# Turning the local q and k in two tiles of five and four tokens, in a sparse attention and expert layer on one core

## The chip, the core and the metric

The kernel runs on one core of one Trainium2 chip. The core has a matrix engine (TensorE, PE in the profile, with its weight loads listed apart as PEld), three engines for elementwise work (VectorE or DVE, ScalarE or ACT, GpSimd or POOL) and an engine that mostly issues transfers (SyncE, SP). Matmuls and transposes write to PSUM, and ACT or DVE copy the result to SBUF. The metric is the device time of one execution in microseconds, the median over several runs; smaller is better.

## The reference

Two layers follow each other. The first is attention over 8 batches, 8 heads, 576 tokens and 64 features a head. Heads 0 to 3 are local (a query sees itself and the 31 keys before it); heads 4 to 7 are strided (a query sees earlier keys at a distance that is a multiple of 32). The second is a two-matmul layer over all 4608 tokens with a leaky activation whose slope `alpha` is given for each of 2048 features.

```python
scores = scale * np.matmul(q, k.transpose(0, 1, 3, 2))
rel = pos[:, None] - pos[None, :]
mask_local = (rel >= 0) & (rel < stride)                      # stride = 32
mask_strided = (rel >= 0) & (pos[None, :] % stride == pos[:, None] % stride)
scores = np.where(masks[None, :, :, :], scores, -1000000000.0)
attn = softmax(scores)
x = np.matmul(attn, v)                                        # heads side by side: (4608, 512)
h = x @ w_in                                                  # (4608, 2048)
g = np.maximum(h, 0.0) + alpha * np.minimum(h, 0.0)
return (g @ w_out).astype(np.float32)                         # (4608, 512)
```

## The kernel before, in words

A batch has four pairs of heads: pairs 0 and 1 are local, pairs 2 and 3 strided. Pair `g` of the whole kernel is pair `g % 4` of batch `g // 4`. For each pair the kernel computes scores (PE), exponentials (ACT), a mask, the product with v (PE, "PV"), a division by the row sum (a reciprocal and a multiplication on DVE), and a transposition of the result into `xT` (PE and a copy, or a DMA). The dense layer then works through nine chunks of 512 tokens: `lin1_piece` (L601: four matmuls of 512 columns into a buffer `hps`, a `neg` on ACT at L609, a `gT` on DVE at L612), and the second matmul (L640, L726, or `U` and `W` at L884 and L899 for the first chunk).

To compute scores, q and k have to lie with the features on the partitions, so they are turned. The local q and k of a batch arrive with nine consecutive tokens on each of 64 partitions per head half, are cast to 16 bit (`cast_l`), and are turned in one of two ways. Batches 0 to 4 use PE: nine transposes each, from one token of two heads each, in `transpose_piece` (L254, called `T(u, nm)`). Later batches use a DMA. The strided q and k go another way (`turn_first`, `turn_second`, or a DMA).

In `transpose_piece` eight tokens go into one PSUM tile `tp` of 2 KB a partition. The destination interleaves tokens: token `9 p + t` is column `9 p + t`, so a copy of eight tokens writes runs of eight adjacent columns and leaves one out. The ninth tokens of q and of k go together into a second tile, `tt`, after k's eight, and are copied by `tails` (L283): q's by DVE, k's by ACT. In batches 0 and 1 (`early`) the eight-token copy is cut by head pair in two halves for ACT and DVE; in batches 2 to 4 it is one ACT copy.

PSUM tiles come from pools with a fixed number of buffers in rotation. The pool `ps` has three, and `tp`, `tt`, the PV results, the turned outputs `xp` and some score tiles all take from it in program order; a new tile waits until the readers of the tile three places before it are done. The pool `hps` has three more, `sp` one.

Each engine works in the order in which the program records its instructions. For batch 0 and batch 1 this order is written out by hand as lists of small pieces (L843 and L910). `F` turns the strided q or k of a pair, `Sc(g, i)` computes half the scores of pair `g`, `Pv(g, a)` one group of PV, `X(g)` the transposition into `xT`, `T` the turn of the local q or k, `Cl` its cast on POOL, `vs` the cast of strided v, `ov` a copy inside the local v, `L(m)` the first half of a `lin1` piece, `w(n)` a number of warm-up matmuls that compute nothing (L768). From batch 2 on, attention pieces are fed one by one between the matmuls of the dense layer (L928), at a rate worked out from what is left.

Of the kernel before, what the change touches and what calls it, by code (L numbers as in the profile page):

```python
# [10 lines left out]
F16 = mybir.dt.float16  # L11
# [21 lines left out]
def kernel(  # L33
# [10 lines left out]
    nc = tc.nc  # L44
    keep = tc.keep_in_program_order
# [17 lines left out]
    pspool = ctx.enter_context(tc.tile_pool(name="ps", bufs=3, space=bass.MemoryType.PSUM))  # L63
# [10 lines left out]
    ident = consts[:, 0:128]  # L74
# [10 lines left out]
    qTs = [cpool.tile([128, 2, 672], F16, name=f"qT{i}") for i in range(2)]  # L85
    kTs = [cpool.tile([128, 2, 672], F16, name=f"kT{i}") for i in range(2)]
# [8 lines left out]
    cast16 = {}  # L95
# [109 lines left out]
    def cast_copy(eng, o, i):  # L205
        if eng == "act":
            keep(nc.scalar.copy(o, i))  # L207
        elif eng == "dve":
            keep(nc.vector.tensor_copy(o, i))  # L209
        else:  # L210
            keep(nc.gpsimd.tensor_copy(o, i))  # L211
# [9 lines left out]
    def over_v(b, eng, c0=0, c1=24):  # L221

        v16 = vls[b % 2]
        a = max(c0, 1)
        cast_copy(eng, v16[0:32, a:c1, :], v16[96:128, a - 1 : c1 - 1, :])
# [28 lines left out]
    def transpose_piece(u, nm):  # L254

        b = u // 2  # L260
        early = b < NEARLY
        src = cast16[(b, False, nm)]
        dst = qTs[u % 2][:, :, 0:576] if nm == "q" else kTs[u % 2][:, :, 32:608]
        tp = pspool.tile([128, 8, 64, 2], F16, tag="ps", name="tp")
        for t in range(8):
            keep(nc.tensor.transpose(
                tp[:, t].rearrange("r p e -> r (p e)"), src[:, t].rearrange("p f d -> p (f d)"), ident))
        main = tp.rearrange("r t p e -> r e p t")
        o = dst.rearrange("r e (p t) -> r e p t", t=9)[:, :, :, 0:8]
        if early:  # L270
            for e in range(2):
                eng = "dve" if (nm == "q") == (e == 0) else "act"
                if u == 0 and nm == "q":
                    eng = "act"
                if nm == "k" and e == 1:
                    tails(b, u)
                cast_copy(eng, o[:, e : e + 1], main[:, e : e + 1])
            return
        cast_copy("act", o, main)
        if nm == "k":  # L280
            tails(b, u)

    def tails(b, u):  # L283
        tt = pspool.tile([128, 2, 64, 2], F16, tag="ps", name="tt")
        for i, nm in enumerate("qk"):
            keep(nc.tensor.transpose(
                tt[:, i].rearrange("r p e -> r (p e)"),
                cast16[(b, False, nm)][:, 8].rearrange("p f d -> p (f d)"), ident))
        for i, (o, eng) in enumerate(((qTs[u % 2][:, :, 0:576], "dve"), (kTs[u % 2][:, :, 32:608], "act"))):
            cast_copy(eng, o.rearrange("r e (p t) -> r e p t", t=9)[:, :, :, 8],  # L290
                      tt[:, i].rearrange("r p e -> r e p"))

    def score_piece(P, i):

# [149 lines left out]
    def x_piece(P, eng):  # L444
        xp = pspool.tile([128, 1024], F16, tag="ps", name="xp")
        for t in range(P.n):
            keep(nc.tensor.transpose(  # L447
                xp[:, P.w * t : P.w * t + P.w], P.x16[0 : P.w, 128 * t : 128 * t + 128], ident[0 : P.w, 0 : P.w]))
# [44 lines left out]
    for g in range(7, npair + 2):  # L493
        c = g // 4
        a, p, t = g, g - 1, g + 1
# [269 lines left out]
    def warm(n):  # L765

        for _ in range(n):
# [12 lines left out]
            name=nc.get_next_instruction_name(), act_func_set_id=6, ins=[], outs=[]  # L780
# [35 lines left out]
    def F(nm, pr):  # L816
        return lambda: turn_first(nm, pr)
# [18 lines left out]
    def L(m):  # L836
        return lambda: lin1_piece(0, m, True)
# [3 lines left out]

    warm(17)
    for fn in [  # L843
        F("q", 0), w(1), F("k", 0), w(2), F("k", 1), Sc(2, 0), w(1), Sc(2, 1), alpha, w(1), F("q", 1), w(2),
        vs(0, 0), vs(0, 1), w(1), Pv(2, 0), Cl(0, "q"), Sc(3, 0), Pv(2, 2), Cl(0, "k"), Pv(2, 1), Sc(3, 1),
        Pv(3, 0), T(0, "q"), w(1), Pv(3, 2), w(1), X(2), T(0, "k"), w(1), Pv(3, 1), w(1), ov(0, "pool", 0, 12),
        Sc(0, 0), Sc(0, 1), X(3), Pv(0, 0), ov(0, "dve", 12, 24), Sc(1, 0), Pv(0, 1), Sc(1, 1), Pv(1, 0), L(0),
        Pv(1, 1), L(3), L(2), X(0, "act"), X(1), L(1)]:
        fn()
    load_d(1)  # L850
    load_v(1, True)
# [27 lines left out]
    def U(kf):  # L879
        def run():  # L880
            if kf == 0:
                banks.extend(phpool.tile([128, 512], F32, tag="hps", name="ops") for _ in range(3))
            for mt in range(3):
                keep(nc.tensor.matmul(  # L884
                    banks[mt], gTs[0][:, kf, 128 * mt : 128 * mt + 128], wout16[:, kf, :],
                    start=(kf == 0), stop=(kf == 15)))
            if kf == 15:
                for mt in range(3):
                    osb = opool.tile([128, 512], F32, tag="osb", name="osb")
                    cast_copy("dve" if mt == 1 else "act", osb, banks[mt])  # L890
                    keep(nc.sync.dma_start(out[128 * mt : 128 * mt + 128, :], osb))
        return run
# [14 lines left out]
    def sc1(g):  # L907
        return lambda: score_both(pairs[g], "dve")

    for fn in [  # L910
        U(0), Cl(1, "q"), G("k", 1), vs(1, 0), vs(1, 1), sc1(6), U(1), U(2), sc1(7), U(3), U(4), Cl(1, "k"), loads2,
        Pv(6, 0), Pv(7, 0), Pv(6, 2), U(5), Pv(7, 1), U(6), T(2, "q"), Pv(7, 2), U(7), T(2, "k"), U(8), Pv(6, 1),
        X(7, "dve"), W(0), W(1), sc1(4), U(9), W(2), sc1(5), W(3), ov(1, "dve", 0, 24), W(4), U(10), X(6), U(11),
        Pv(4, 1), W(5), Pv(4, 0), U(12), Pv(5, 1), U(13), U(14), Pv(5, 0), U(15), W(6), X(5), X(4), W(7)]:
        fn()
# [65 lines left out]
```

## Time and profile before

| what | value |
| --- | --- |
| median of 3 runs | 307.54 us (306.44, 307.66, 307.54) |
| profiled execution | 306.46 us, its span 304.5 us |
| PE busy | 294.4 us (97% of the span) |
| DVE, ACT, POOL busy | 223.4, 176.1, 175.6 us |
| granted clock of PE | 1.000 |
| batch 0's dense run of L601 begins | 24.96 us |

Times in the profile count from the start of the span. A row of the timeline has a start, a duration, the engine, the line and operation, the output and inputs, their shape and a count; behind it in brackets stands how long the engine was idle before it and what ended that wait. A row of the waits has an engine and its line, what it waited for, and total, number and longest in microseconds. A matmul's row ends when its result is in PSUM, by a model; the next matmul can start well before that.

### The profile page before, as it was taken

Reading aid. Unit: us, or ns where it says so; the run is one execution under the profiler, and the core shown is the slowest. Engines: PE = TensorE matmul, PEld = TensorE weight load, DVE = VectorE, ACT = ScalarE, POOL = GpSimd, SP = SyncE. Lnnn points to the kernel's source line nnn. Section 1 sums busy time; section 2 is a strip of 40 time slices with the busy share of each in tenths; the row PEclk is TensorE's granted clock in tenths of the full one; section 3 lists DMA queues with packets and bytes.
Section 4 is the critical chain, followed back from the end, with each engine's and each line's share of the span. In section 5 each row is a group of like instructions: output and inputs, shape, how many; then the busy total and the mean of one; then the engine's idle time right before and its main releaser. Section 6 shows DMA issues by size and latency. Waiting matters only on the chain.

```text
span 304.5 us, 6839 instructions
## 1 busy us (share of the span) xinstructions
PE 294.4 (97%) x2688; PEld 182.3 (60%) x2688; DVE 223.4 (73%) x413; ACT 176.1 (58%) x326; POOL 175.6 (58%) x163
## 2 busy tenths in 40 slices
PE   8989998999999998999999999999999999999995
PEld 3654454544555466845874587457745974685484
DVE  4567897758875888478948894889489948935852
ACT  1485744388557775577357746774575446426630
POOL 8362274128959997979897989394744404002300
PEclk9999999999999999999999999999999999999999
DMA  7999999999999998999989999955920040022003
GB/s 185 256 194 197 263 176 259 136 209 328 90 173 169 112 104 83 135 210 123 145 127 204 141 141 169 194 86 94 189 56 19 6 156 2 0 69 71 1 2 138
DMA packets 96976, 41.18 MB, mean 135 GB/s; under 512 B 75360, under 2 KB 93232, under 8 KB 96944
## 3 DMA queue, kind: packets, MB, share of 16 engines
q0 software_dynamic: 51008, 17.77, 57.3%
q1 hardware_dynamic: 45584, 22.32, 32.9%
q10 hardware_dynamic: 352, 0.66, 0.8%
q8 instruction: 21, 0.34, 0.5%
q14 instruction: 11, 0.09, 0.1%
HBM read 38.24 MB, written 9.44 MB: 157 GB/s over the span
## 4 chain that ended last, share of the span: by engine, by line
PE 79%; DVE 10%; ACT 6%; issue 2%; DMA 2%; SPq 0%; DVEq 0%; ACTq 0%
PE hps L601 36%; PE ops L726 24%; PE ops L640 4%; PE pv L424 4%; DVE gT L612 3%; DVE gsum L670 2%; PE sp L371 2%; PE ops L884 2%; DMA consts<-consts 2%; ACT neg L609 2%; DVE qT L209 1%; PE sph L371 1%; PE xp L447 1%; ACT kT L207 1%; PE ops L899 1%
## 5 line engine op out<-in xcount | busy, mean ns | idle before, releaser
L601 PE MATMUL hps<-xT,win 128*128 128x512 f16 x576 | 131.9, 379 | 0.2 <-ACT xT L470 0.2
L612 DVE SCALAR_TENSOR_TENSOR gT<-neg,oma,hps 128x512 f16<-128x512 f32 x144 | 105.3, 744 | 36.4 <-ACT neg L609 28.5
L609 ACT ACTIVATE neg<-hps 128x512 f32<-128x512 f32 x144 | 86.3, 601 | 34.7 <-PE hps L601 32.7
L601 PEld LDWEIGHTS <-win 128*128 128x128 f16 x576 | 53.8, 98 | 59.2 <-issue 0.7
L396 POOL TENSOR_TENSOR et<-et,consts 128x576 f16<-128x576 f16 (+1 forms) x24 | 34.7, 1447 | 35.4 <-ACT et L394 35.1
L670 POOL TENSOR_TENSOR gsum<-gT 128x1024 f16<-128x1024 f16 x14 | 29.7, 2124 | 42.2 <-DVE gT L612 37.2
L726 PEld LDWEIGHTS <-gsum 128*128 128x128 f16 x448 | 40.9, 98 | 7.3 <-DVE gsum L670 2.1
L726 PE MATMUL ops<-wsum,gsum 128*128 128x256 f16 x328 | 41.6, 273 | 0.4 <-DVE gsum L670 0.2
L726 PEld LDWEIGHTS <-gT 128*128 128x128 f16 x336 | 31.5, 98 | 5.4 <-issue 0.3
L433 DVE TENSOR_TENSOR x<-pv,rc 96x384 f16<-96x384 f32 (+2 forms) x62 | 33.0, 532 | 2.1
L403 POOL TENSOR_TENSOR et<-et,consts 128x576 f16<-128x576 f16 (+1 forms) x24 | 31.5, 1311 | 0.0
L424 PEld LDWEIGHTS <-et 72*128 72x128 f16 (+1 forms) x448 | 23.2, 98 | 12.5 <-issue 1.8
L726 PE MATMUL ops<-wout,gT 128*128 128x256 f16 x224 | 27.9, 272 | 0.1
L394 ACT ACTIVATE et<-sp 128x576 f16<-128x576 f32 (+1 forms) x24 | 15.6, 648 | 16.6 <-PE sp L371 16.6
L431 DVE RECIPROCAL rc<-pv 96x6 f32<-96x6 f32 (+2 forms) x80 | 14.6, 183 | 10.2 <-PE pv L424 10.2
L681 DVE TENSOR_TENSOR osb<-ops,par 128x512 f32<-128x512 f32 (+1 forms) x14 | 9.4, 672 | 16.1 <-PE ops L726 8.2
L400 ACT ACTIVATE et<-sph 128x288 f16<-128x288 f32 (+1 forms) x48 | 19.0, 413 | 0.0
L679 ACT COPY osb<-ops 128x512 f32<-128x512 f32 x14 | 8.2, 586 | 17.0 <-PE ops L726 16.9
L211 POOL COPY vs<-stv 72x1024 f16<-72x1024 f16 x12 | 13.4, 1118 | 6.7 <-DMA stv<-in_v_dram 6.7
L640 PE MATMUL ops<-wout,gT 128*128 128x512 f16 x64 | 16.4, 379 | 0.0
L424 PE MATMUL pv<-vs,et 72*128 72x65 f16 x256 | 15.2, 193 | 0.8 <-DVE vs L209 0.7
L743 ACT COPY par<-ops 128x512 f32<-128x512 f32 x13 | 8.0, 612 | 13.5 <-PE ops L726 13.5
(109 smaller groups left out, 342.2 us busy)
## 6 DMA issues: line engine op xcount, KB each, us to landing
out_dram<-osb SPq DMA_DIRECT2D x35, 256.0 KB, 3.4
vl<-in_v_dram POOLq DMA_DIRECT2D x6, 384.0 KB, 8.8
win<-in_moe_w_in_dram POOLq DMA_DIRECT2D x4, 512.0 KB, 16.8
wout<-in_moe_w_out_dram POOLq DMA_DIRECT2D x4, 512.0 KB, 17.7
qsd<-in_q_dram POOLq DMA_DIRECT2D x7, 288.0 KB, 5.9
ksd<-in_k_dram POOLq DMA_DIRECT2D x7, 288.0 KB, 7.0
stv<-in_v_dram POOLq DMA_DIRECT2D x7, 288.0 KB, 7.1
ql<-in_q_dram SPq DMA_DIRECT2D x3, 576.0 KB, 6.2
```

The source lines that it names most:

```text
L394: keep(nc.scalar.activation(ev.rearrange("r (y c) -> r y c", y=2), sp[0:r, :, 0:n], AF.Exp, scale=SCALE))
L396: keep(nc.gpsimd.tensor_tensor(mv, mv, m, op=ALU.mult))
L400: keep(nc.scalar.activation(ev[:, n * y : n * y + n], sps[y][0:r, 0:n], AF.Exp, scale=SCALE))
L403: keep(nc.gpsimd.tensor_tensor(mv, mv, m, op=ALU.mult))
L424: keep(nc.tensor.matmul(pv[:, 65 * x : 65 * x + 65], et[0:r, c : c + 128], v16[0:r, 2 * P.pr + hh, t, :] if P.strided else v16[:, 6 * (2 * ...
L433: keep(nc.vector.tensor_tensor(P.x16[0:w, c0 : c0 + 64 * nb].rearrange("r (c e) -> r c e", e=64), pvv[:, :, 0:64], rc[0:w, 0:nb].unsqueeze ...
L601: keep(nc.tensor.matmul(hps, win16[:, kk, 128 * m : 128 * m + 128], xT[:, kk, c0 : c0 + 512], start=(kk == 2), stop=(kk == 1)))
L609: keep(nc.scalar.activation(neg, hps, AF.Relu, scale=-1.0))
L612: keep(nc.vector.scalar_tensor_tensor(gTs[n][:, m, :], neg, oma[:, m : m + 1], hps, op0=ALU.mult, op1=ALU.add))
L640: keep(nc.tensor.matmul(ops, gTs[n][:, kf, 128 * mt : 128 * mt + 128], wout16[:, kf, :], start=(kf == 0), stop=(kf == 15)))
L670: keep((nc.vector if eng == "dve" else nc.gpsimd).tensor_tensor(gsum[i][:, hs], a, b, op=op))
L726: keep(nc.tensor.matmul(o, lhs(y), rhs(y), start=(first and y == 0), stop=(y == 7), skip_group_check=True))
```

## The change

Only the turn of the local q and k, and the written-out orders, are changed. `transpose_piece` now makes two `tp` tiles for each of q and k: the first holds tokens 0 to 4, the second tokens 5 to 8. Each tile is copied with one instruction, for both head pairs. The first copy is always ACT's. The second is ACT's too, except in batches 0 and 1, where DVE makes it (but ACT for the q of batch 0). `tails` and its tile `tt` are gone.

The list of batch 0 has another order, and seven warm-up matmuls between its pieces where there were twelve. In it v is cast earlier (`vs`), the score halves of pairs 3, 0 and 1 come in another order, `T(0, "k")` comes ahead of `Pv(2, 1)`, `X(3)` and `X(2)`, and X(2) and X(3) change places. In batch 1 one PV piece and `U(8)` change places.

```diff
-        tp = pspool.tile([128, 8, 64, 2], F16, tag="ps", name="tp")
-        for t in range(8):
-            keep(nc.tensor.transpose(
-                tp[:, t].rearrange("r p e -> r (p e)"), src[:, t].rearrange("p f d -> p (f d)"), ident))
-        main = tp.rearrange("r t p e -> r e p t")
-        o = dst.rearrange("r e (p t) -> r e p t", t=9)[:, :, :, 0:8]
-        if early:
-            for e in range(2):
-                eng = "dve" if (nm == "q") == (e == 0) else "act"
-                if u == 0 and nm == "q":
-                    eng = "act"
-                if nm == "k" and e == 1:
-                    tails(b, u)
-                cast_copy(eng, o[:, e : e + 1], main[:, e : e + 1])
-            return
-        cast_copy("act", o, main)
-        if nm == "k":
-            tails(b, u)
-
-    def tails(b, u):
...
+        o = dst.rearrange("r e (p t) -> r e p t", t=9)
+        tps = []
+        for t0, t1 in ((0, 5), (5, 9)):
+            tp = pspool.tile([128, 8, 64, 2], F16, tag="ps", name="tp")
+            for t in range(t0, t1):
+                keep(nc.tensor.transpose(
+                    tp[:, t - t0].rearrange("r p e -> r (p e)"), src[:, t].rearrange("p f d -> p (f d)"), ident))
+            tps.append(tp[:, 0 : t1 - t0].rearrange("r t p e -> r e p t"))
+        cast_copy("act", o[:, :, :, 0:5], tps[0])
+        cast_copy("dve" if early and (u or nm == "k") else "act", o[:, :, :, 5:9], tps[1])
...
-        F("q", 0), w(1), F("k", 0), w(2), F("k", 1), Sc(2, 0), w(1), Sc(2, 1), alpha, w(1), F("q", 1), w(2),
-        vs(0, 0), vs(0, 1), w(1), Pv(2, 0), Cl(0, "q"), Sc(3, 0), Pv(2, 2), Cl(0, "k"), Pv(2, 1), Sc(3, 1),
-        Pv(3, 0), T(0, "q"), w(1), Pv(3, 2), w(1), X(2), T(0, "k"), w(1), Pv(3, 1), w(1), ov(0, "pool", 0, 12),
-        Sc(0, 0), Sc(0, 1), X(3), Pv(0, 0), ov(0, "dve", 12, 24), Sc(1, 0), Pv(0, 1), Sc(1, 1), Pv(1, 0), L(0),
-        Pv(1, 1), L(3), L(2), X(0, "act"), X(1), L(1)]:
+        F("q", 0), w(1), F("k", 0), w(1), F("k", 1), Sc(2, 0), vs(0, 0), w(1), F("q", 1), Sc(2, 1), alpha, Pv(2, 0),
+        Sc(3, 1), vs(0, 1), Cl(0, "q"), Cl(0, "k"), Pv(2, 2), Sc(3, 0), w(1), Pv(3, 2), T(0, "q"), Pv(3, 0), w(1),
+        Pv(3, 1), w(1), T(0, "k"), X(3), w(1), Sc(0, 1), Pv(2, 1), Sc(0, 0), Sc(1, 1), ov(0, "dve", 12, 24),
+        ov(0, "pool", 0, 12), Pv(0, 1), X(2), Pv(0, 0), Sc(1, 0), Pv(1, 1), L(1), X(0, "act"), Pv(1, 0), L(2), L(3),
+        X(1), L(0)]:
...
-        Pv(6, 0), Pv(7, 0), Pv(6, 2), U(5), Pv(7, 1), U(6), T(2, "q"), Pv(7, 2), U(7), T(2, "k"), U(8), Pv(6, 1),
+        Pv(6, 0), Pv(7, 0), Pv(6, 2), U(5), Pv(7, 1), U(6), T(2, "q"), Pv(7, 2), U(7), T(2, "k"), Pv(6, 1), U(8),
```

More of the change, by code (lines that the diff above doesn't have):

```diff
@@ L263, in transpose_piece @@
         dst = qTs[u % 2][:, :, 0:576] if nm == "q" else kTs[u % 2][:, :, 32:608]
-        tp = pspool.tile([128, 8, 64, 2], F16, tag="ps", name="tp")
-        for t in range(8):
-            keep(nc.tensor.transpose(
-                tp[:, t].rearrange("r p e -> r (p e)"), src[:, t].rearrange("p f d -> p (f d)"), ident))
-        main = tp.rearrange("r t p e -> r e p t")
-        o = dst.rearrange("r e (p t) -> r e p t", t=9)[:, :, :, 0:8]
-        if early:
-            for e in range(2):
-                eng = "dve" if (nm == "q") == (e == 0) else "act"
-                if u == 0 and nm == "q":
-                    eng = "act"
-                if nm == "k" and e == 1:
-                    tails(b, u)
-                cast_copy(eng, o[:, e : e + 1], main[:, e : e + 1])
-            return
-        cast_copy("act", o, main)
-        if nm == "k":
-            tails(b, u)
-    def tails(b, u):
[L284 to L291, printed above, removed]
+        o = dst.rearrange("r e (p t) -> r e p t", t=9)
[8 more added lines that the diff above has]
+        cast_copy("dve" if early and (u or nm == "k") else "act", o[:, :, :, 5:9], tps[1])
     def score_piece(P, i):
```

## The prediction

> **What bounds the kernel now.** I read the page's first part, then the waits of TensorE alone, then the timeline around each of the five places where the local q and k are turned.
>
> ```profile
> span 304.5 us, 6839 instructions
> PE 294.4 (97%) x2688; PEld 182.3 (60%) x2688; DVE 223.4 (73%) x413; ACT 176.1 (58%) x326; POOL 175.6 (58%) x163
> ...
> PE 79%; DVE 10%; ACT 6%; issue 2%; DMA 2%; SPq 0%; DVEq 0%; ACTq 0%
> ```
>
> TensorE (PE) is busy for 97% of the span, and the other engines are not close to full. So only two things save time: less matmul work, or an end to a stall of PE. The waits of PE name the stalls (total, times, longest, in us):
>
> ```profile
> PE sp L371 <- ACT kT L207: 1.6, 3, 0.8
> ...
> PE sp L313 <- ACT kT L207: 1.0, 1, 1.0
> PE pv L424 <- DVE vs L209: 0.7, 1, 0.7
> PE xp L447 <- ACT kT L207: 0.7, 1, 0.7
> PE tt L286 <- ACT qT L207: 0.5, 1, 0.5
> ```
>
> Apart from the `vs` row, each of these waits ends at a copy out of a transpose tile, and these are the copies that the change rewrites. The groups of those copies (min/median/max in ns):
>
> ```profile
> L207 ACT COPY qT<-tp x6: 588/800/1016, 16.0 to 112.9; 128x512 f16<-128x512 f16 x3, 128x1024 f16<-128x1024 f16 x3
> L207 ACT COPY kT<-tt x5: 718/722/737, 18.6 to 118.7; 128x128 f16<-128x128 f16 x5
> L209 DVE COPY qT<-tt x5: 710/715/726, 17.9 to 118.0; 128x128 f16<-128x128 f16 x5
> L209 DVE COPY qT<-tp x1: 678/678/678, 46.3 to 46.3; 128x512 f16<-128x512 f16 x1
> ```
>
> A ninth token's copy moves 128 elements a partition and takes 0.72 us, more than the 0.59 us of 512 elements in runs of eight. It writes single 2-byte elements 18 bytes apart. So the price here is not by elements alone.
>
> **The price of one new copy.** It writes 128 runs (2 x 64) of five or four elements. Below stands the ninth token's copy, 128 runs of one at 0.72 us; above stands the old big copy, 128 runs of eight at 1.01 us. By elements alone, from 0.59 us at 512 and 1.01 at 1024 (0.82 ns each), 640 would take 0.69 and 512 would take 0.59 us. I take 0.75 us for either, since the ninth token's row has the same count of runs and lies nearest; the ends are 0.59 and 1.01. The same on DVE, whose row for the ninth token is 0.71.
> [...]
>
> **Batches 2 to 4 (one turn each).** Before, after k's eight transposes, three copies follow each other, the last two on one shared tile: k's eight tokens (ACT), q's ninth (DVE), k's ninth (ACT). The first scores wait for the last.
>
> ```profile
> 65.64 1.89 PE L601 MATMUL hps<-xT,win 128*128 128x512 f16 x8
> 65.78 1.01 ACT L207 COPY kT<-tp 128x1024 f16<-128x1024 f16 x1
> 67.32 0.72 ACT L207 COPY kT<-tt 128x128 f16<-128x128 f16 x1 [0.54 <-DVE qT L209]
> 68.09 0.30 PE L371 MATMUL sp<-qT,kT 64*128 64x96 f16 x6 [0.56 <-ACT kT L207]
> ...
> 85.93 1.01 ACT L207 COPY kT<-tp 128x1024 f16<-128x1024 f16 x1 [1.34 <-PE tp L266]
> 86.83 1.03 PE L640 MATMUL ops<-wout,gT 128*128 128x512 f16 x4
> 88.05 0.30 PE L371 MATMUL sp<-qT,kT 64*128 64x96 f16 x6 [0.19 <-ACT kT L207]
> ...
> 116.53 1.02 ACT L207 COPY kT<-tp 128x1024 f16<-128x1024 f16 x1
> 117.63 1.04 PE L726 MATMUL ops<-wsum,gsum 128*128 128x256 f16 x8
> 118.71 0.72 ACT L207 COPY kT<-tt 128x128 f16<-128x128 f16 x1 [1.16 <-DVE qT L209]
> 119.48 0.30 PE L371 MATMUL sp<-qT,kT 64*128 64x96 f16 x6 [0.82 <-ACT kT L207]
> ```
>
> A matmul row includes the last one's modelled tail, so a 512-wide matmul takes (1.89 - 0.38) / 7 = 0.216 us of PE, a 256-wide one (1.04 - 0.27) / 7 = 0.11. PE could have gone on at 65.64 + 8 x 0.216 = 67.37, at 86.83 + 4 x 0.216 = 87.69 and at 117.63 + 8 x 0.11 = 118.50. It went on at 68.09, 88.05 and 119.48: stalls of 0.72, 0.36 and 0.98, in sum 2.06 us. After, k's two ACT copies start where the one started and end 1.5 us on, at 67.3, 87.4 and 118.0, each ahead of the moment when PE is free. So all 2.06 us go. At 1.01 a copy they end at 67.8, 87.95 and 118.55, and 0.3 + 0.1 + 0.9 = 1.3 is left, less perhaps 0.3 for ACT work that queues behind q's copies.
> What it adds: ACT has 4 x 0.75 = 3.0 us a batch where it had 1.01 + 1.01 + 0.72 = 2.74, and DVE loses 0.71. ACT is at 58%, so the 0.26 us lie beside matmuls; the `neg` evictions behind q's copies come at most 0.5 us later, which the three rotating `hps` buffers cover (0.87 us of matmuls each). The eighteen transposes stay eighteen: zero. With these waits gone, the next thing late is a PV wait on DVE's eviction in batch 4, which stays.
>
> **Batch 1.**
>
> ```profile
> 46.32 0.68 DVE L209 COPY qT<-tp 128x512 f16<-128x512 f16 x1
> 47.03 0.59 ACT L207 COPY qT<-tp 128x512 f16<-128x512 f16 x1 [3.81 <-DVE qT L209]
> 47.67 0.22 PE L286 MATMUL tt<-consts,ql 128*128 128x128 f16 x1 [0.47 <-ACT qT L207]
> ...
> 48.33 0.89 DVE L209 COPY kT<-tp 128x512 f16<-128x512 f16 x1
> 48.74 0.72 ACT L207 COPY kT<-tt 128x128 f16<-128x128 f16 x1 [0.63 <-DVE qT L209]
> 49.51 0.42 PE L447 MATMUL xp<-consts,x 72*128 72x72 f16 x8 [0.74 <-ACT kT L207]
> ```
>
> Here ACT and DVE shared one tile and went one after the other. PE stalled twice: for the buffer of `tt`, and for that of `xp`. After, ACT takes five tokens and DVE four from different tiles, side by side. DVE still frees q's second tile first at 46.3 + 0.75 = 47.1, so k's second tile costs PE some 0.2 us. The PV piece that now stands ahead of U(8) takes its buffer from the one evicted behind that copy, some 0.4 us more. ACT is through with k's first tile by 48.0, so `xp` starts at about 48.6 and not 49.51: 0.9 us. Ends: 0.3 (copies of 1.01, two of them in DVE's queue) and 1.2 (both waits gone).
>
> **Batch 0.**
>
> ```profile
> 14.06 1.15 POOL L211 CAST kl<-kl 128x1152 f16<-128x1152 f32 x1 [1.00 <-DMA kl<-in_k_dram]
> 17.12 0.64 ACT L207 COPY xT<-xp 128x576 f16<-128x576 f16 x1
> 17.13 0.61 PE L266 MATMUL tp<-consts,kl 128*128 128x128 f16 x8
> 19.04 0.17 DVE L431 RECIPROCAL rc<-pv 72x6 f32<-72x6 f32 x1
> 19.24 0.55 DVE L433 TENSOR_TENSOR x<-pv,rc 72x384 f16<-72x384 f32 x1
> 19.41 0.30 PE L313 MATMUL sp<-qT,kT 64*128 64x96 f16 x6 [0.95 <-ACT kT L207]
> 24.96 11.04 PE L601 MATMUL hps<-xT,win 128*128 128x512 f16 x50
> ```
>
> The new order puts X(2) and PV(2,1) behind k's turn. K is cast at 14.06 + 1.15 = 15.2, so its transposes can stand at about 15.6 instead of 17.13 (q's two ACT copies free the buffer about then). With ACT's five tokens and DVE's four side by side, 0.75 each behind DVE's eviction of the last strided PV, kT is whole at some 17.1, and the first local scores stand there instead of at 19.41: 2.3 us earlier. The moved X(2) then costs ACT 0.64 us between there and the dense run; PV(2,1), 0.17 + 0.55 on DVE, has slack there, and is the lower end. That leaves 1.7, and 1.6 after the last X copy's wait. Ends: 2.3 (nothing moved counts) and 0.7 (PV counts, and some 0.2 of waits). The earlier `vs` cast stands ahead of q's second strided copy on DVE, so a late v would hold that copy and the scores behind it:
>
> ```profile
> 1.43 1.56 POOL L189 DMA_DIRECT2D stv<-in_v_dram  x2 [0.27 <-issue]
> ...
> DMA to landing us min/median/max: 8.5/9.1/9.7
> ```
>
> The first half lands at 1.43 + 8.5 = 9.9 us, about when DVE is ready for it; the second at about 12.0, by its place before the next eviction. Five warm-up matmuls fewer take 5 x 0.216 = 1.1 us of PE work out; it lay in stalls, so it counts nothing by itself. SP and POOL issue the same transfers in the same order, and POOL's own casts wait for landings that do not move.
>
> **The sum.** 1.6 + 0.9 + 2.06 = 4.6 us. Nothing behind these places gives it back by the profile: in the stages after 128 us PE runs without such waits and only shifts. The profiled execution took 306.46 us (span 304.5 and 2.0 around it): 301.9. The median of the runs shown is 307.54, 1.1 more: 303.0, which I predict.
>
> **The rivals.**
> *Dear copies.* Runs of four and five cost what runs of eight do, 1.01 us. For it: the ninth token's row shows a price by run. Against it: the row lies at the lower end. Gain 0.7 to 1.6 + 0.3 + 1.0, about 2.4: 305.1 us. Chance 0.12.
> *Batch 0 gives nothing*, because another wait (v, or ACT's exps) takes the place. Gain 2.9: 304.6. Chance 0.06.
> *A cold clock.* The opening shows PE at half rate:
>
> ```profile
> 5.01 0.15 PEld L768 LDWEIGHTS <-wrm 128*128 128x128 f16 x1 [0.28 <-issue]
> 5.43 1.22 PEld L768 LDWEIGHTS <-wrm 128*128 128x128 f16 x6 [0.28 <-issue]
> ```
>
> Starts are 5.43 - 5.01 = 0.42 us apart there, then 0.2. With fewer warm-up matmuls the clock could fall back for a spell as long as that opening, some 4 us, at about 1.7 us of cost beyond the stalls: 304.7. Against it: PE never stalls for over 1 us in the prologue. Chance 0.04. [...]
> *Slower: the ring of three `ps` buffers.* Each turn now holds two of three at once, and twice in a batch; before, a batch took three tiles, now four. If PE stood at the second tile of each of the ten turns for the copy (0.75) and its signals, some 1.0 us, that is 10 us against 4.6: 313 us. It decides from 0.5 us a turn. For it: PE already waits for `tt`'s buffer in batch 1. Against it: in batches 2 to 4 other matmuls lie between the pieces, and the buffers' last readers end before. Chance 0.12.
>
> **How the numbers follow.** The forecast has 0.66. A measurement of this kernel can tell about 0.5%, 1.5 us. The first three rivals are still faster by that; slower is the ring; the same gets 0.04, taken from the dear copies. So faster 0.84, same 0.04, slower 0.12. The range goes from 301.2 (all upper ends: 2.3 + 1.2 + 2.06 = 5.6, and the base 0.8 lower) to 306.0, which leaves out the ring, and the dear copies where they meet a poor batch 0.
>
> **What would show it.** The changed profile has no `tt`, twenty ACT or DVE copies from `tp` near 0.75 us, no wait of `sp` on `kT` above 0.2 us in batches 2 to 4, the first dense run of L601's work near 23.4 to 24.1 us, and `xp` of batch 1 some 2.5 us earlier than 49.51. Copies near 1.0 us, new PE waits on `tp`, or POOL waits that eat the shift would make it wrong.

## The result and the profile after

The changed kernel takes 303.27 us (median of 5 runs, 302.57 to 303.51); the kernel before, run beside it, takes 307.44 us (306.44 to 307.66). The ratio is 0.987, with a 95% interval of 0.984 to 0.989: faster by 1.3%, with the whole interval below 1. The predicted time was 303.0 us. The two profiled executions are closer to each other than the medians: 306.46 us before (span 304.5) and 303.51 us after (span 301.5), a difference of 3.0 us against 4.2 between the medians. The trace can explain only the 3.0.

Lines behind the turn have moved up by 18: L583 is the dense matmul that was L601, L353 the scores of L371, L406 the PV of L424, L373 the mask of L391. Three lines of the changed kernel's page, the span, the engines' busy time (with share of the span and instructions) and the chain by engine:

```profile
span 301.5 us, 6823 instructions
...
PE 293.3 (97%) x2683; PEld 181.8 (60%) x2683; DVE 220.8 (73%) x408; ACT 175.5 (58%) x327; POOL 175.8 (58%) x163
...
PE 80%; DVE 10%; ACT 4%; issue 3%; DMA 2%; SPq 0%; ACTq 0%; DVEq 0%
```

ACT's share of the chain has gone from 6% to 4%, DVE's has stayed at 10%. The waits of TensorE in the changed kernel (total, times, longest, in us) show what went:

```profile
PE pv L406 <- DVE x L415: 0.9, 2, 0.7
PE tf L153 <- DVE id L779: 0.6, 1, 0.6
PE pv L406 <- ACT qT L207: 0.5, 1, 0.5
PE pv L406 <- DVE vl L209: 0.5, 1, 0.5
PE xp L429 <- DVE x L415: 0.3, 1, 0.3
```

All waits of scores on `kT` (2.6 us before) are gone, and so are those of `tt` and `xp` on ACT's copies (1.2 us). Four lines are new, PV behind DVE's `x` and `vl` and behind ACT's `qT`, and `xp` behind `x`: 2.2 us in sum. The wait on `id` has grown from 0.2 to 0.6 us; `id` itself waits for a transfer in the opening (DVE's row of `id` at 7.13, 2.15 us). The copies of the turn in the changed kernel (ns, min/median/max) cost 0.71 to 0.76 us whether they move five tokens or four:

```profile
L207 ACT COPY qT<-tp x9: 718/748/757, 14.4 to 111.3; 128x640 f16<-128x640 f16 x5, 128x512 f16<-128x512 f16 x4
L207 ACT COPY kT<-tp x8: 727/752/762, 16.3 to 115.1; 128x640 f16<-128x640 f16 x5, 128x512 f16<-128x512 f16 x3
L209 DVE COPY kT<-tp x2: 710/714/718, 16.8 to 47.1; 128x512 f16<-128x512 f16 x2
L209 DVE COPY qT<-tp x1: 714/714/714, 45.3 to 45.3; 128x512 f16<-128x512 f16 x1
```

The timeline of the changed kernel at the five turns answers to the rows of the prediction. No score matmul has a wait behind it. In batch 1 a PV piece now stands 0.49 us for a buffer that q's first copy holds, where `tt` and `xp` together stood 1.21 us before:

```profile
16.80 0.71 DVE L209 COPY kT<-tp 128x512 f16<-128x512 f16 x1
17.66 0.30 PE L295 MATMUL sph<-qT,kT 64*128 64x96 f16 x6
...
45.64 0.28 PE L406 MATMUL pv<-vs,et 72*128 72x65 f16 x4 [0.49 <-ACT qT L207]
...
47.74 0.42 PE L429 MATMUL xp<-consts,x 72*128 72x72 f16 x8
...
64.69 1.36 ACT L207 COPY kT<-tp 128x640 f16<-128x640 f16 x2
66.33 0.30 PE L353 MATMUL sp<-qT,kT 64*128 64x96 f16 x6
...
86.00 0.30 PE L353 MATMUL sp<-qT,kT 64*128 64x96 f16 x6
...
116.53 0.30 PE L353 MATMUL sp<-qT,kT 64*128 64x96 f16 x6
```

Where the time went is seen from the start of the same work in five kernels (us from the start of the span; the last three columns belong to experiments below):

| place on PE | before | changed | new turn alone | new orders alone | changed, casts on ACT |
| --- | --- | --- | --- | --- | --- |
| batch 0, first local scores | 19.41 | 17.66 | 20.20 | 17.54 | 17.21 |
| dense run of 50 matmuls | 25.13 | 23.35 | 25.87 | 23.28 | 22.95 |
| batch 1, first transpose of q | 45.38 | 44.35 | 46.12 | 44.12 | 43.17 |
| batch 1, first local scores | 50.73 | 48.96 | 50.73 | 49.47 | 47.78 |
| batch 2, first local scores | 68.09 | 66.33 | 67.89 | 66.83 | 64.50 |
| batch 3, first local scores | 88.05 | 86.00 | 87.57 | 86.76 | 84.17 |
| batch 4, first local scores | 119.48 | 116.53 | 118.09 | 118.17 | 114.70 |
| end of the span | 304.5 | 301.5 | 303.1 | 303.9 | 299.7 |

The dense run's start is that of the chain of work that ended last. In the timeline it begins 0.16 to 0.17 us earlier in each of the five (24.96 and 23.18 in the first two).

The lead of the changed kernel over the one before goes 1.75, 1.78, 1.03, 1.77, 1.76, 2.05, 2.95, 3.0. Batch 0 gives 1.8 and batch 1's turn 0.74 (1.77 - 1.03). Batches 2 to 4 give 1.8: the lead grows by 0.29 in batch 3 and 0.90 in batch 4, and by 0.63 in batch 2, where it stood at 1.13 just ahead of the turn. Twice lead is lost: 0.75 between the dense run and batch 1's first transpose, and 0.64 between batch 1's scores and the second chunk of the dense layer (which starts at 59.19, 60.32 before). The places sum to 4.4 us, and 1.4 us is given back.

Both losses lie where DVE masks the exponentials of batch 1 (L391 before, L373 after: two inputs, both in SBUF) while POOL casts a local input (L211). The kernel before in the timeline:

```profile
39.37 1.15 POOL L211 CAST ql<-ql 128x1152 f16<-128x1152 f32 x1 [6.91 <-DMA ql<-in_q_dram]
40.73 1.40 POOL L211 CAST kl<-kl 128x1152 f16<-128x1152 f32 x1 [0.22 <-DMA kl<-in_k_dram]
41.05 2.66 DVE L391 TENSOR_TENSOR et<-et,consts 72x576 f16<-72x576 f16 x4
...
51.76 1.06 DVE L391 TENSOR_TENSOR et<-et,consts 128x576 f16<-128x576 f16 x2 [1.03 <-ACT et L385]
53.36 1.18 DVE L391 TENSOR_TENSOR et<-et,consts 128x576 f16<-128x576 f16 x2 [0.54 <-ACT et L385]
```

The changed kernel in the same view:

```profile
38.82 0.90 DVE L373 TENSOR_TENSOR et<-et,consts 72x576 f16<-72x576 f16 x2
40.86 1.90 DVE L373 TENSOR_TENSOR et<-et,consts 72x576 f16<-72x576 f16 x2 [1.13 <-ACT et L367]
41.31 1.14 POOL L211 CAST kl<-kl 128x1152 f16<-128x1152 f32 x1 [0.58 <-DMA kl<-in_k_dram]
43.51 0.36 PE L406 MATMUL pv<-vs,et 72*128 72x65 f16 x6 [0.71 <-DVE x L415]
...
49.99 1.06 DVE L373 TENSOR_TENSOR et<-et,consts 128x576 f16<-128x576 f16 x2 [0.83 <-ACT et L367]
51.63 1.77 DVE L373 TENSOR_TENSOR et<-et,consts 128x576 f16<-128x576 f16 x2 [0.58 <-ACT et L367]
51.63 1.47 POOL L211 CAST ql<-ql 128x1152 f16<-128x1152 f32 x1 [4.22 <-DMA ql<-in_q_dram]
54.04 0.36 PE L406 MATMUL pv<-vl,et 128*128 128x65 f16 x6 [0.47 <-DVE vl L209]
```

A pair of masks takes 0.90 and 1.06 us alone, but 1.90 and 1.77 where a cast runs. The casts wait for a landing, so they do not move up (41.31 where 40.73 was, 51.63 where 50.84 was), while the masks have moved up with the matmuls. How much is lost depends on how the two meet: in the kernel before, a cast from 52.72 to 53.87 overlapped the pair at 53.36, which took only 0.12 us more. PE then stands 0.71 and 0.47 us at a PV behind DVE. That the cast beside them is what makes the masks longer was still to be tested.

### The profile page after: what moved, and what is told of

It is laid out like the page before. It is cut to its first block, busy times and chain, and to the rows that moved or that the text cites. A ratio compares the mean times of both kernels' runs of the same rounds, so it can differ in the third digit from the quotient of the medians.

```text
span 301.5 us, 6823 instructions
## 1 busy us (share of the span) xinstructions
PE 293.3 (97%) x2683; PEld 181.8 (60%) x2683; DVE 220.8 (73%) x408; ACT 175.5 (58%) x327; POOL 175.8 (58%) x163
## 4 chain that ended last, share of the span: by engine, by line
PE 80%; DVE 10%; ACT 4%; issue 3%; DMA 2%; SPq 0%; ACTq 0%; DVEq 0%
PE hps L583 35%; PE ops L708 25%; PE ops L622 5%; PE pv L406 4%; DVE gT L594 3%; PE ops L866 2%; DVE x L415 2%; PE sp L353 2%; DMA consts<-consts 2%; ACT neg L591 2%; DVE gsum L652 2%; PE xp L429 1%; PE sph L353 1%; PE tp L269 1%; PE ops L881 1%
## 5 line engine op out<-in xcount | busy, mean ns | idle before, releaser
L583 PE MATMUL hps<-xT,win 128*128 128x512 f16 x576 | 131.9, 379 | 0.2 <-ACT xT L452 0.2
L583 PEld LDWEIGHTS <-win 128*128 128x128 f16 x576 | 53.7, 98 | 59.2 <-issue 0.5
L406 PEld LDWEIGHTS <-et 72*128 72x128 f16 (+1 forms) x448 | 23.3, 98 | 13.1 <-issue 1.8
L413 DVE RECIPROCAL rc<-pv 96x6 f32<-96x6 f32 (+2 forms) x80 | 14.6, 183 | 10.4 <-PE pv L406 10.2
L406 PE MATMUL pv<-vs,et 72*128 72x65 f16 x256 | 15.4, 193 | 1.7 <-DVE x L415 0.9
L211 POOL COPY vs<-stv 72x1024 f16<-72x1024 f16 x12 | 13.3, 1116 | 6.3 <-DMA stv<-in_v_dram 6.3
```

The lines of the kernel that those rows point to most:

```text
L406: keep(nc.tensor.matmul(pv[:, 65 * x : 65 * x + 65], et[0:r, c : c + 128], v16[0:r, 2 * P.pr + hh, t, :] if P.strided else v16[:, 6 * (2 * ...
L583: keep(nc.tensor.matmul(hps, win16[:, kk, 128 * m : 128 * m + 128], xT[:, kk, c0 : c0 + 512], start=(kk == 2), stop=(kk == 1)))
```

## The experiments

The theory after the traces has three parts: the copies go at one price per run of adjacent columns; the gain of batches 1 to 4 comes from the new turn and that of batch 0 from the order; and the masks that meet POOL's casts give 1.4 us back. The rivals: batch 0's gain comes from copies side by side; the warm-up matmuls that were taken out are what counts; five and four is a better cut than eight and one; the second copies on ACT hold the path. The twelve kernels ran in three groups, each on one chip beside runs of the kernel before (306.67 us in the first group, 306.88 in the second, 306.55 in the third). Kernels of different groups are therefore compared by their ratios. The expectations of the first group took the kernel before at about 307.4 us, so there the gain says more than the time.

### The new turn alone

```diff
 # transpose_piece as changed; the lists of batches 0 and 1 as before
```

> The new turn in the old written-out orders of batches 0 and 1. Theory A (the turn carries most): batch 0's kT is whole about 0.8 us earlier than 19.41 (one ACT copy and one DVE copy in place of three in a row), batch 1 keeps about 0.9 and batches 2 to 4 about 2.1, so 3.8 less what is lost on the way: 303.6 to 304.6 us. Theory B (the new order carries batch 0 and through it the gain): under 2 us of gain, 305.5 to 306.5 us. Copies from tp near 0.75 us in both.

Measured: 304.73 us (304.45 to 305.04), ratio 0.993 (0.991 to 0.995): between the two expected ranges, and a gain of 1.9 us, which theory B had as under 2. In the table, batch 0 gains nothing, its dense run even begins 0.74 later than before; batch 1's turn gains the same 0.74 as in the changed kernel, and from batch 1's scores to the end 1.4 us are gained. The profile shows one reason why batch 0 is late in this execution. Windows of the timeline of this kernel (us, then busy time and instructions of PE, PEld, DVE, ACT and POOL, the clock granted to PE, DMA share, GB/s):

```profile
13.10:16.50 3.40, 2.50 (x51) 1.94 (x52) 3.07 (x10) 1.57 (x4) 1.46 (x2) 1.00 2.11 156
16.50:19.90 3.40, 3.40 (x35) 2.54 (x32) 1.65 (x4) 2.33 (x4) 3.38 (x5) 0.51 1.24 204
```

For 3.4 us, PE had half its clock (0.51). Such a fall is what the prediction's third rival reckoned with, and it stands here in another kernel. It is not what sets the median: the mean granted clock was 0.994 in this execution and 1.000 in the three others, of which one took 304.99 us and two 304.5. The timeline of the same kernel shows PE waiting for DVE's copy into `vs` ahead of the half clock:

```profile
13.84 0.34 PE L406 MATMUL pv<-vs,et 72*128 72x65 f16 x6 [1.10 <-DVE vs L209]
```

### The new orders alone

```diff
 # transpose_piece and tails as before; the lists of batches 0 and 1 as changed
```

> The new orders with the old turn (eight tokens and a ninth). Theory A: the dense run of batch 0 begins about 1 us earlier than 24.96 (its kT waits for three copies in a row as before), and part of that is lost in batch 1 again, so 306.3 to 307.0 us. Theory B: 1.5 us or more of gain by the order alone, 305.0 to 305.9 us.

Measured: 305.78 us (305.25 to 306.31), ratio 0.997 (0.996 to 0.998): the time lies in theory B's range, but the gain of 0.9 us is less than B's 1.5. The orders alone bring the dense run to 23.28, as early as in the changed kernel (23.35). So batch 0's gain is there without the new copies. Of this lead of 1.85 us, 0.59 is lost ahead of batch 1's first transpose, where here too a pair of masks beside a cast takes 1.73 us. A lead of 1.3 lasts through batch 4 (the stalls of batches 2 to 4 are the old ones), and then half is lost in the dense layer. The kernel with the orders alone, in the timeline:

```profile
17.54 0.30 PE L313 MATMUL sph<-qT,kT 64*128 64x96 f16 x6 [0.93 <-ACT kT L207]
...
188.18 0.69 ACT L207 COPY xT<-xp 128x192 f16<-128x192 f16 x2
188.54 0.81 PE L601 MATMUL hps<-xT,win 128*128 128x512 f16 x3 [0.60 <-ACT xT L207]
```

At 188.54 PE waits 0.60 us for a copy into `xT`, which no other kernel here shows. The two halves alone give 1.9 and 0.9 us by the medians, 2.8 in sum, somewhat less than the 3.0 to 4.2 of both. In the profile of the orders alone the 0.60 us would account for the gap to the lower of these; whether this wait stands in every execution was not shown.

### The turn alone with PE kept busy

```diff
-alpha, w(1), F("q", 1), w(2),
+alpha, w(1), F("q", 1), w(6),
```

(against the kernel with the new turn alone)

> The turn alone (old orders) with four more warm-up instructions in batch 0, placed where TensorE stood idle for 1.1 us before the half clock of the run of the turn alone (304.73 us). If the half clock between 16.5 and 20 us of that run is what ate batch 0's gain, and the short idle stretch brought it on: TensorE's mean granted clock 1.0, the dense run of L583 at 24.2 to 25.0 in place of 25.87, total 303.8 to 304.5. If the half clock does not hang on that stretch: the clock stays near 0.99, total 304.5 to 305.0. If the clock is mended but the turn by itself gives nothing in batch 0 (the old order's wait for the matmuls of the first pieces decides): the dense run near 25.1, total 304.3 to 304.8.

Measured: 304.42 us (304.08 to 304.87), ratio 0.992 (0.990 to 0.995). The same windows of this kernel have the full clock:

```profile
13.10:16.50 3.40, 2.84 (x54) 2.02 (x53) 3.07 (x10) 1.65 (x4) 1.85 (x3) 1.00 2.11 156
16.50:19.90 3.40, 3.07 (x46) 1.79 (x45) 2.31 (x6) 2.27 (x4) 3.21 (x5) 1.00 1.25 205
```

The clock was full in all four executions. That the four matmuls did this is not shown, since three of the four executions without them had it too, and the medians differ by 0.3 us in two groups. What the profile does show is batch 0 with the new turn, the old order and a full clock: its dense run begins at 24.78 by the chain, 0.35 ahead of the kernel before, of which 0.23 stands already at the first strided transposes (7.09 and 7.32). Some 0.1 us is left for the turn and the four matmuls together. By batch 1's first transpose (45.43, before 45.38) the lead is gone; the four masks ahead of it take 2.50 us beside casts. By the numbers this is the first expectation; in what it says of the turn it is the third.

### The casts of batches 1 and 2 on ACT

```diff
-        U(0), Cl(1, "q"), G("k", 1), ..., sc1(7), U(3), U(4), Cl(1, "k"), loads2,
+        U(0), G("k", 1), ..., sc1(7), Ca(1, "q"), Ca(1, "k"), U(3), U(4), loads2,
...
-        cast_l(2, "q")
-        cast_l(2, "k")
...
-        ... X(6), U(11),
+        ... X(6), Ca(2, "q"), Ca(2, "k"), U(11),
```

> The changed kernel, with the four casts of the local q and k of batches 1 and 2 on ACT instead of POOL (behind the exponentials of the pairs before them). In the changed profile a pair of DVE masks of batch 1 takes 1.90 us at 40.86 and 1.77 us at 51.63, where the undisturbed pairs take 0.90 and 1.06, each time beside a POOL cast. Theory C (the masks stand still while POOL casts, and this is where 0.8 and 0.6 us of the lead of batch 0 and 1 are given back): both pairs at about 1.0 us, the first matmul of the second chunk about 1.2 to 1.4 us earlier than 59.19, time 302.0 to 302.5 us. Theory D (the lead is lost to something else that follows the landing of transfers): no change of the time beyond 0.3 us, 303.0 to 303.5.

Measured: 301.54 us (301.47 to 301.62), ratio 0.983 (0.981 to 0.985), the best of all kernels here and lower than theory C had it. It is 1.7 us below the first median of the changed kernel; by the ratios (0.987 and 0.986 for the changed kernel) it is 1.1 to 1.2, and by the profiled spans 1.8. The masks of this kernel in the timeline are at their price alone:

```profile
38.42 0.90 DVE L373 TENSOR_TENSOR et<-et,consts 72x576 f16<-72x576 f16 x2
40.45 1.05 DVE L373 TENSOR_TENSOR et<-et,consts 72x576 f16<-72x576 f16 x2 [1.14 <-ACT et L367]
...
48.81 1.06 DVE L373 TENSOR_TENSOR et<-et,consts 128x576 f16<-128x576 f16 x2 [0.83 <-ACT et L367]
50.45 1.06 DVE L373 TENSOR_TENSOR et<-et,consts 128x576 f16<-128x576 f16 x2 [0.58 <-ACT et L367]
```

From the dense run to batch 1's first transpose it takes 20.22 us, the changed kernel 21.00; from batch 1's scores to batch 2's 16.72 against 17.37; from there to the end 235.2 in both. So the collisions cost 0.78 + 0.65 = 1.43 us, which is what the traces had as given back. The other 0.40 us of the span lie ahead of the dense run and are not the casts': 0.35 of them stand already at the first strided transposes (7.03 here, 7.38 in the changed kernel, where PE waits 0.61 us for `id`, which waits for a transfer).

### The same casts on ACT in the kernel before

```diff
 # the edit above, in the kernel before
```

> The kernel before with the same four casts on ACT. Theory C: the four masks at 41.05 took 2.66 us with a POOL cast beside them and would take about 1.9, so 0.7 us of gain at most, 306.6 to 307.1 us, less than in the changed kernel, whose second pair of masks was hit too. Theory D: no change, 307.2 to 307.6.

Measured: 306.15 us (305.89 to 307.30), ratio 0.999 (0.997 to 1.000): not clear of no change, and no 0.7 us. In the profile the four masks take 0.81 + 1.05 us in place of 2.66, yet batch 1's first transpose starts at 45.34, where the kernel before has 45.38. From the dense run to there the kernel before took 20.25 us, as little as the changed one without collisions: its long masks hid behind other work. The collision is paid for only where the matmuls come early enough to wait for it.

### The changed kernel again

> The changed kernel once more, as the base of the runs beside it: 302.5 to 303.5 us. If the 1 us between its own runs follows the landing of transfers, its profile differs from the first one in the start of the first strided transposes (7.38 there) or in the masks beside POOL's casts (1.90 and 1.77 us there), and nowhere else.

Measured: 303.22 us (302.64 to 303.43), ratio 0.986 (0.983 to 0.990). In this profile the masks took 1.68 and 1.23 us where the first one had 1.90 and 1.77. The second loss is there all the same (batch 1's scores to batch 2's take 17.72 us, 16.72 without collisions), but it has another carrier: DVE's copy inside the local v, 0.54 us in the first profile, takes 1.44 beside the next cast, and PE waits 0.83 us for it.

```profile
52.40 1.15 POOL L211 CAST kl<-kl 128x1152 f16<-128x1152 f32 x1 [0.61 <-DMA kl<-in_k_dram]
52.50 1.44 DVE L209 COPY vl<-vl 32x1495 f16<-32x1495 f16 x1
```

So not only masks take longer: in this execution a cast that waited for its landing met a copy of DVE's. The runs of the changed kernel lie 0.8 us apart, those of the kernel with its casts on ACT 0.15. That the landings make this spread fits both, but was not shown run by run.

### The five warm-up matmuls put back

```diff
-w(1), F("k", 1), Sc(2, 0), vs(0, 0), w(1), F("q", 1), ... Sc(3, 0), w(1), Pv(3, 2), ... Pv(3, 0), w(1), ... X(3), w(1),
+w(2), F("k", 1), Sc(2, 0), vs(0, 0), w(2), F("q", 1), ... Sc(3, 0), w(2), Pv(3, 2), ... Pv(3, 0), w(2), ... X(3), w(2),
```

> The changed kernel with the five warm-up matmuls put back into its batch 0 (twelve as before). Theory A (they lay in stalls of PE and count nothing): within 0.4 us of the changed kernel beside it, the dense run of batch 0 at most 0.4 us later. Theory E (PE bounds the new prologue, their 1.1 us come back): 0.8 to 1.1 us slower. The granted clock is 1.0 throughout in both.

Measured: 303.51 us (302.72 to 303.74), ratio 0.988 (0.984 to 0.991); the clock was full with and without them. The dense run began at 23.98, 0.8 us later than in the run beside it (23.17), and batch 1's first transpose 0.63 later, yet the total differs by no more than 0.3 us. Of the 0.8 us, 0.30 stand already at the first strided transposes (7.74 and 7.44). So some 0.5 of the 1.1 us of the five matmuls lie on the path of batch 0 (0.3 against the first profile of the changed kernel), and the rest in stalls: between the two expectations.

### Eight and one in tiles of their own

```diff
-        for t0, t1 in ((0, 5), (5, 9)):
+        for t0, t1 in ((0, 8), (8, 9)):
...
-        cast_copy("act", o[:, :, :, 0:5], tps[0])
+        cast_copy("act", o[:, :, :, 0:8], tps[0])
```

> The new code with its two tiles cut as eight tokens and one instead of five and four; q's and k's ninth tokens have their own tiles and copies. Theory F (most of the gain of batches 2 to 4 comes from the end of the shared tile and of the row of three copies, not from five and four): the copies take 1.01 and 0.72 us, k's chain ends 0.25 us later than with 0.75 twice, and the time is 0.1 to 0.6 us above the changed kernel. Theory G (the equal halves carry the gain): 1.5 us or more above it, since the longer first copy puts the waits back.

Measured: 303.31 us (302.71 to 303.94), ratio 0.987 (0.984 to 0.991), as the changed kernel. The tile's copies of this kernel:

```profile
L207 ACT COPY kT<-tp x8: 730/1014/1044, 16.4 to 114.6; 128x1024 f16<-128x1024 f16 x5, 128x128 f16<-128x128 f16 x3
```

A turn costs 1.01 + 0.73 = 1.74 us of copies, 0.24 more than five and four, and two waits of scores on `kT` come of it: 0.43 us in batch 0 and 0.21 in batch 2. The total does not show them; in this profile the first pair of masks met no cast (1.05 us), which can hide as much. The gain of batches 1 to 4 is that q and k no longer meet in a tile and in a row of three copies, since it stays with eight and one; the cut itself is worth nothing that these medians can tell.

### The second copies always on DVE

```diff
-"dve" if early and (u or nm == "k") else "act"
+"dve" if not early or u or nm == "k" else "act"
```

> The second copy always on DVE, also in batches 2 to 4. Theory A (k's chain no longer sets the first scores there): within 0.4 us of the changed kernel, although k's copies end 0.7 us sooner. Theory H (PE still waits for k in batches 2 to 4): 0.3 to 0.8 us faster.

Measured: 303.34 us (303.20 to 304.38), ratio 0.988 (0.985 to 0.992), no change in the total. But see the next kernel.

### Casts on ACT and second copies on DVE

```diff
 # both edits: the casts of batches 1 and 2 on ACT, every second copy but one on DVE
```

> The changed kernel with the four casts of the local inputs of batches 1 and 2 on ScalarE and, besides, every second copy (but batch 0's of q) on VectorE in batches 2 to 4 too. If the second copies of batches 2 to 4 are off the path, as the run with them on VectorE alone had it: 301.3 to 301.8, as with the casts alone (301.54). If ScalarE is the tighter engine once it has the casts: 300.6 to 301.2.

Measured: 302.48 us (302.19 to 302.85), ratio 0.986 (0.984 to 0.989): 0.9 above the casts alone (which ran in another group), outside both expectations. Up to batch 4 the two kernels run within 0.02 us of each other. This one then loses 0.87 us in batch 4 (scores at 115.57, 114.70 with the casts alone). Its timeline there:

```profile
110.54 1.76 DVE L652 TENSOR_TENSOR gsum<-gsum,gT 128x1024 f16<-128x1024 f16 x1
...
112.22 0.72 DVE L209 COPY qT<-tp 128x512 f16<-128x512 f16 x1
...
112.99 0.38 PE L269 MATMUL tp<-consts,kl 128*128 128x128 f16 x4 [0.55 <-DVE qT L209]
...
115.57 0.30 PE L353 MATMUL sp<-qT,kT 64*128 64x96 f16 x6
```

The copy stands in DVE's queue behind a sum of 1.76 us, so that k's second tile waits for q's buffer. The kernel that had only the second copies on DVE shows the same wait (0.55 us at 113.79), but in its profile batch 2's scores started at 65.35, 0.98 us ahead of the changed kernel's 66.33. There the first masks had met no cast for long (1.10 us). At batch 4's scores 0.16 of that lead is left, so its unchanged total hides a loss in batch 4. ACT is the right engine for the second copy there.

### Three tiles of three tokens

```diff
-        for t0, t1 in ((0, 5), (5, 9)):
+        for t0, t1 in ((0, 3), (3, 6), (6, 9)):
...
+        cast_copy("act", o[:, :, :, 3:6], tps[1])
```

> Three tiles of three tokens with a copy each (two on ScalarE, the third where the second was). By the run: each copy 0.70 to 0.75 us, so one ScalarE copy of 0.72 more per batch and tensor, and a third tile from the ring of three that serves both tensors: q's tiles and k's tiles would each fill the ring, so k's first transposes wait for q's copies; total 303.5 to 306. By the element: copies of 0.45 to 0.5, total 302.5 to 303.5. If the ring of three buffers is what bounds (the slower rival of the prediction), the transposes of k show waits of over 0.5 us for each of the batches and the total is over 305.

Measured: 306.68 us (305.50 to 309.21), ratio 1.001 (0.998 to 1.004), above what both prices gave. Three of its ten executions had a mean granted clock of 0.983 and took 308.9 to 309.2 us; the seven at full clock took 305.5 to 307.0. The profile is of one of the three. Copies, waits of PE, and windows of this kernel:

```profile
L207 ACT COPY qT<-tp x14: 718/738/766, 14.2 to 116.1; 128x384 f16<-128x384 f16 x14
```

```profile
PE tp L269 <- DVE x16s L416: 1.2, 1, 1.2
PE tp L269 <- ACT qT L207: 0.8, 2, 0.4
PE tp L269 <- ACT kT L207: 0.5, 1, 0.5
```

```profile
11.40:14.85 3.45, 2.76 (x41) 1.76 (x42) 3.08 (x8) 2.47 (x7) 2.03 (x2) 1.00 1.69 251
14.85:25.25 10.40, 9.81 (x100) 6.65 (x100) 4.89 (x13) 6.34 (x13) 5.96 (x9) 0.51 1.32 196
```

Three things are seen. The copy of 384 elements costs 0.74 us, as much as one of 640 in the changed kernel (0.75); both write 128 runs. The ring of three buffers now holds PE, 2.5 us over four waits, which is the prediction's slower rival in a kernel where a turn fills the ring. And in this execution PE lost half its clock for some 10.2 us (0.51 in the mean of the 10.40 above), so that the dense run began at 27.39, 4.0 us after the changed kernel's.

### Copies that write whole runs of 64 columns

```diff
-        o = dst.rearrange("r e (p t) -> r e p t", t=9)
+        o = dst.rearrange("r e (t p) -> r e t p", t=9)
...
-            tps.append(tp[:, 0 : t1 - t0].rearrange("r t p e -> r e p t"))
+            tps.append(tp[:, 0 : t1 - t0].rearrange("r t p e -> r e t p"))
```

> The changed kernel with the two copies writing whole runs of 64 columns in place of runs of four or five columns that lie nine apart: the same tokens land in other columns, so that attention works on keys and queries in another order of tokens, in the same number of operations. Price by the length of the run that is written: 320 and 256 elements per partition per half go at about 1.08 ns each, so 0.69 and 0.55 to 0.59 us on ScalarE in place of 0.75 and 0.75. Price by element whatever the run: unchanged, 0.71 to 0.76. Total 302.3 to 303.5 by either.

Measured: 303.49 us, one run. The copies of this kernel:

```profile
L207 ACT COPY qT<-tp x9: 591/686/693, 14.3 to 111.1; 128x640 f16<-128x640 f16 x5, 128x512 f16<-128x512 f16 x4
L209 DVE COPY kT<-tp x2: 677/684/692, 16.6 to 46.7; 128x512 f16<-128x512 f16 x2
```

With long runs an ACT copy takes 0.59 us for 512 elements and 0.69 for 640. The interleaved write costs some 0.15 and 0.06 us on top. The order of reading from PSUM changes along with the order of writing, but it does not set the price: the kernel before reads in the same jumps as the changed one, writes runs of eight, and takes 0.59 us for 512 elements too. The total does not move: some 0.1 us a copy, once the stalls are gone, lies beside matmuls.

## Why the prediction was right, and where it was not

**The price of a copy.** Taken 0.75, measured 0.71 to 0.76. The choice of the ninth token's row as the nearest was right, and its reason too: runs of one cost 0.72 us, of three 0.74, of four and five 0.71 to 0.76. Two copies back to back are through after 1.36 us (the row at 64.69), not after the 1.5 of the prediction, since the second begins (65.3) before the first ends (0.75 after 64.69). By elements alone, four tokens would have taken 0.59; measured 0.72 to 0.75 on ACT, so that price fails here. It would not have changed the time, as the long runs show (303.49 us).

**Batches 2 to 4.** Forecast 2.06 us, measured 0.63 + 0.29 + 0.90 = 1.8. The mechanism holds: all waits of `sp` on `kT` are gone, and with the orders alone all stand as before. Each place gave about 0.1 us less than its stall.

**Batch 1.** Forecast 0.9, measured 0.74, both where the new turn runs with the old orders and where it runs with the new. The two old waits of 0.47 and 0.74 are gone; one of 0.49 has come, at the PV piece between the turns. The prediction had 0.2 at k's second tile and 0.4 at a later PV piece, where PE does not wait: the size is nearly right, the place is not. The signal named for it, `xp` some 2.5 us earlier than 49.51, came 1.77 earlier: 0.75 of the lead from batch 0 had been lost ahead of it.

**Batch 0.** Forecast 1.6, measured 1.8 (dense run from 24.96 to 23.18 in the timeline; 23.4 to 24.1 was named). The size is nearly right, one of its reasons is not: "With ACT's five tokens and DVE's four side by side" brings nothing here, since the orders alone reach 23.28 by the chain with the old copies, and the changed kernel 23.35. And "it lay in stalls, so it counts nothing by itself" was wrong of the warm-up matmuls: put back, they move the dense run by 0.3 to 0.5 us beyond the delay that stands already at the first strided transposes. Which other piece of the new order gives the rest of the gain was not tried piece by piece.

**The step that failed.** "Nothing behind these places gives it back by the profile", with "POOL's own casts wait for landings that do not move" a little above it. The second sentence is true as far as it matters (the casts came 0.2 to 0.9 us later, none earlier) and contains the cause: DVE's masks moved up into them, and 1.4 us of 4.4 were lost. The casts on ACT get them back. The prediction counted POOL as a queue and not as an engine beside whose casts DVE takes longer (1.90 us for a pair of masks, 1.05 with the casts on ACT). Its last paragraph names "POOL waits that eat the shift" as a sign of being wrong, but the sum has no term for it.

**The number.** Against the profiled execution the sum was 4.6 and 3.0 us came. The time of 303.0 came within 0.3 us of the median all the same, because the medians differ by 4.2: the runs of the kernel before spread over 1.2 us, and its profiled execution lies at their lower end. Its 307.44 us is itself high, for the 39 runs of it in the three groups have medians of 306.55 to 306.88; beside the second set of runs of the changed kernel the gain is 3.7. Part of the closeness is luck.

**The rivals.** Dear copies: no, 0.75 us. Batch 0 gives nothing: true of the new turn alone, not with the new order. The cold clock: in none of the nine runs of the changed kernel (granted clock 0.999 to 1.000), but in some executions of two neighbours of it (0.51 for 3.4 and some 10.2 us in the two profiles). The kernel before had a lower mean in some executions too: six of those 39 runs had 0.993 or 0.994 and took 307.0 to 308.5 us, the other 33 took 306.1 to 307.4; where in them the clock was lower was not shown. The opening, from whose half pace this rival took its 4 us, reads a granted clock of 1.00 (0 to 5 us of the kernel before), so that it is the same thing was not shown. The ring of three: no wait of PE on `tp` in the changed kernel, and only the one PV piece of 0.49 us waits for a buffer that a turn holds; for more it takes a third tile a turn. The 1.0 us for a copy and its signals that this rival took was the author's estimate; no wait on a turn's copy in the changed kernel is longer than the 0.49.

## What to carry to other kernels

When a change moves PE's work up, look at what does not move with it: here POOL's casts, which wait for landings, came 0.2 to 0.9 us later and none earlier, and the masks that moved up ran into them, at 1.4 us. Where a copy writes short interleaved runs, look at its runs and not only at its elements (128 runs took 0.71 to 0.76 us here, with 128 elements or with 640), and split two results that share a tile and a row of copies before tuning their sizes (eight and one took 303.31 us, five and four 303.22). Look at the granted clock of every execution and not only of the profiled one: the kernel with three tiles had 0.983 in three of its ten executions and 1.000 in the other seven.

## What the runs showed of the hardware

- An ACT copy from PSUM that wrote 2-byte elements in 128 runs, which begin 18 bytes apart, took 0.72 to 0.75 us (medians) whether a run had one, three, four or five elements. With 128 runs of eight it took 1.01 us for 1024 elements, and with long runs 0.59 us for 512 and 0.69 for 640.
- A pair of DVE masks with both inputs in SBUF took 0.6 to 0.85 us longer where POOL casts of 1.15 to 1.5 us ran beside most of it, and 0.12 and 0.17 where about half of one did. With the casts on ACT the four pairs of batch 1 took 0.90 to 1.06 us. A DVE copy of 0.54 us took 1.44 where it began beside such a cast.
- The clock granted to PE fell to half (0.50) in some executions and not in others of the same kernel. In the 3.4 us ahead of the two profiled falls PE was busy 2.50 of 3.40 and 2.76 of 3.45 us, and its longest wait there was 1.10 us in the first and 0.38 us in the second. The clock stayed at 1.00 with 2.84 of 3.40, but also in the kernel before with 2.30 of 3.40 (16.50 to 19.90 us), so the busy share alone does not decide. The falls lasted some 3.4 and 10.2 us. What brings a fall on, and what ends it, was not shown.
